# Loads of a sketched attention and channel mix: weights ahead, v pieces of batches 1 and 2 between halves of the next batch's keys and queries

## The chip, the cores and the metric

The kernel runs on one core of one Trainium2 chip, in one launch. Its time is the device time of an execution in microseconds; a version is told by the median of several executions. One further execution is taken by the hardware profiler, which lists what every engine did and when; the span is the time from its first instruction to its last.

## The reference

Polysketch attention, followed by an RWKV channel mix on its output. There are 4 batches, 4 heads, 1088 positions, a head size of 32; the sketch has 8 rows, so a feature vector has 64 entries.

```python
def phi(x):                                   # S1, S2: 8 x 32
    a = np.einsum('rd,bhsd->bhsr', S1, x)
    b = np.einsum('rd,bhsd->bhsr', S2, x)
    return np.einsum('bhsi,bhsj->bhsij', a, b).reshape(*x.shape[:-1], r * r)
q_p, k_p = (phi(q), phi(k))
kv = np.einsum('bhsf,bhsd->bhfd', k_p, v)     # needs all of k and v of a batch
z = np.sum(k_p, axis=2)
num = np.einsum('bhsf,bhfd->bhsd', q_p, kv)
den = np.einsum('bhsf,bhf->bhs', q_p, z)[..., None] + 1e-06
x = num / den                                 # heads side by side: 4 x 1088 x 128
xk = mu_k * x + (1.0 - mu_k) * x_prev         # x_prev: x one position earlier
xr = mu_r * x + (1.0 - mu_r) * x_prev
k = np.maximum(xk @ w_k, 0.0)                 # w_k: 128 x 1024
v = k * k @ w_v                               # w_v: 1024 x 128
out = 1.0 / (1.0 + np.exp(-(xr @ w_r))) * v   # w_r: 128 x 128
```

Inputs and output are float32.

## The kernel before

The four batches go one after the other through the attention and then through the channel mix, and the stages of different batches are interleaved by hand. The positions of a head are cut into 32 runs of 34 (`U`); with 4 heads that makes the 128 partitions, so a tile of keys or queries of one batch is 128 x (34 x 32). Three things written out as text set the order of the work.

**The loads.** `LOADS` (lines 31 to 34) is a list of entries: what is loaded, `@`, and the queue that issues it (S is SyncE, A is ScalarE). `load` (line 128) turns an entry into DMAs: `k` and `q` of a batch (line 139) go whole, in two halves of 17 columns each, or in the part that `UH` (line 126) names; `v` (line 143) goes in four pieces, `v10` to `v13` for batch 1, each into 32 of the 128 partitions of `vin`; `w0` is `w_k` (line 146), `w1` is `w_v` (line 148), `w2` is `w_r` (line 150). All loads but the four smallest come from the SyncE queue, in the order of the list. The list is issued at line 160, ahead of all compute.

**The order of compute.** `ORDER` (lines 35 to 66) lists every task for all engines; each engine carries out its own tasks in that order. A task has its arguments behind points, `@` gives the PSUM banks that it writes, and the last letter the engine (V VectorE, A ScalarE, G GpSimd, P VectorE reading PSUM). `^` ties a GpSimd task to the end of a VectorE task.

**The tasks that read the loads:**
- `turn.k.b` and `turn.q.b` (line 252) transpose keys and queries on VectorE, 32 x 32 blocks at a time, into `kT` and `qT`, of which there are two each. Batch 0 is turned in two parts; for the keys of batches 1 and 2 (`WHOLE_K`) there are two transposes (line 261); the keys of batch 3 and the queries of batches 1 to 3 are one transpose (line 264), which reads all 34 columns.
- `kproj` (line 268) multiplies the turned keys with the sketch on TensorE (line 274 for batches 1 and 2, line 280 for 0 and 3); `abev` copies it out of PSUM; `kp` (line 298) forms the 64 features.
- `zmm` (line 307), `wmm` (line 315) and `wsq` make the weights of the query projection `abw` (lines 365 to 386).
- `kvmm` (line 327) sums features times v over the positions: the one reader of `vin`.
- `wset.0` (line 244, GpSimd) scales `w_k` into bf16, `wset.1` (line 246) casts `w_v`, `wset.2` (lines 248, 249) scales `w_r`; `wset.2` is tied to the end of `xs.0` on VectorE.
- `xmm` (lines 496, 513) gives the attention's output, `f1` (line 553), `relu`, `sq`, `f2` (line 586), `rr` (line 599), `sig`, `fin` are the channel mix.

Around the two places that read batch 1's v and batch 3's keys, TensorE's list is `kproj.2.0, f1.1.0, kvmm.1, zmm.2, kproj.3.0, kproj.3.1, wmm.2, f1.0.1`, and VectorE's is `turn.q.2, abev.2.1, turn.k.3, kp.2.0, abev.3.1, wsq.2`.

`zz` (line 175) are matmuls on a tile of zeros, whose result nobody reads. The outputs are stored from line 622 and 618.

Of the kernel before, what the change touches and what calls it, by code (L numbers as in the profile page):

```python
# [20 lines left out]
SIGMOID = mybir.ActivationFunctionType.Sigmoid  # L21
# [7 lines left out]
WHOLE_K = (1, 2)  # L29
WHOLE_Q = (0, 1, 2)  # L30
LOADS = """
S0@A S1@S m0@A m1@A k00@S k01@S q01@S q00@S v00@S v01@S v02@S v03@S k1@S q1@S w0@S v10@S v11@S v12@S v13@S w2@S w1@S
k2@S q2@S k3@S q3@S v20@S v21@S v22@S v23@S v30@S v31@S v32@S v33@S
"""
ORDER = """
turn.k.0.0.V smm.0@0 cset.0 turn.k.0.1.V zz.5@7 kproj.0.1@0 abev.0.1.A kproj.0.0@1 turn.q.0.1.V cset.4.G abev.0.0.V
# [37 lines left out]
def kernel(  # L74
# [14 lines left out]
    nc = tc.nc  # L89
    B, H, S, D = q.shape  # L90
# [4 lines left out]
    U = S // 32  # L95
# [14 lines left out]
    kin = [const.tile([P, U * D], F32, name=f"k{b}") for b in range(B)]  # L110

    X32 = [const.tile([P, U + 1, 32], F32, name=f"qx{b}") for b in range(B)]
    qin = [x[:, 1:, :].rearrange("p u d -> p (u d)") for x in X32]
# [9 lines left out]
    omu = const.tile([P, 2], F32, name="omu")  # L123
    rat = const.tile([P, 1], F32, name="rat")
    tmp = const.tile([P, 1], F32, name="tmp")
    UH = {"k": {"": (0, U), "0": (0, 18), "1": (18, U)}, "q": {"": (0, U), "0": (0, 16), "1": (16, U)}}

    def load(what, eng):
        e = nc.sync if eng == "S" else nc.scalar if eng == "A" else nc.gpsimd
        x, b, i = what[0], int(what[1]), what[2:]  # L130
        if x == "S":
            e.dma_start(S16[R * b:R * b + R, :], S2 if b else S1)
        elif x == "m":
            e.dma_start(mu_row[b:b + 1, :], (moe_mu_r if b else moe_mu_k).rearrange("d -> () d"))
        elif x in "kq":
            src = (k if x == "k" else q)[b].rearrange("h (a u) d -> (h a) (u d)", u=U)
            lo, hi = UH[x][i]
            for lo, hi in ((lo, hi),) if i else ((0, U // 2), (U // 2, U)):
                e.dma_start((kin if x == "k" else qin)[b][:, lo * D:hi * D], src[:, lo * D:hi * D])
        elif x == "v":  # L140
            c = int(i)
            u, n = CU[c]
            e.dma_start(vin[b][32 * c:32 * c + 32, :, :n, :].rearrange("p h m d -> p h (m d)"),
                        v[b].rearrange("h (a u) d -> h a u d", u=U)[:, :, u:u + n, :].rearrange("h a m d -> a h (m d)"))
        elif x == "w" and b == 0:
            e.dma_start(wk_f[:, :, :DFF // 2], moe_w_k.rearrange("p (y f) -> p y f", y=2))
        elif x == "w" and b == 1:
            e.dma_start(wv_f[:, :, :DFF // 2], moe_w_v.rearrange("(p y c) d -> p y (c d)", y=2, c=NC // 2))
        else:
            e.dma_start(wr_f[:], moe_w_r)  # L150

    warm = const.tile([R, 1], F32, name="warm")
# [4 lines left out]
    nc.vector.memset(warm[:], 0.0)  # L157
    for b in range(B):
        nc.vector.memset(vin[b][64:, :, 8, :], 0.0)
    for entry in LOADS.split():  # L160
        load(*entry.split("@"))
    nc.scalar.activation(warm[:], warm[:], SIGMOID)


    ident = const.tile([P, P], F32, name="ident")
# [86 lines left out]
    def turn(x, b, y, eng="V"):  # L252
        lo, hi = UH[x][str(y) if y < 2 else ""]
        t, src = (kT, kin) if x == "k" else (qT, qin)
        t = t[b % 2][:].rearrange("p u a -> p (u a)")
        if x == "k" and b in WHOLE_K:

            for c in (0, 2):
                u, n = CU[c]
                if lo <= u < hi:  # L260
                    nc.vector.transpose(_ap(t, [[32, 2], [P, n], [1, 32]], 32 * c),
                                        src[b][:, D * u:D * (u + 2 * n)].rearrange("p (c m d) -> p c m d", c=2, m=n))
        else:
            nc.vector.transpose(t[:, 32 * lo:32 * hi], src[b][:, D * lo:D * hi])  # L264
# [412 lines left out]
```

## Time and profile before

| | us |
|---|---|
| three executions | 82.67, 80.83, 82.23 |
| their median | 82.23 |
| the profiled execution, its own time | 81.55 |
| its span in the profile | 79.8 |

Busy time in the span: TensorE 73.0 us (91%), weight loads 54.1, VectorE 64.0 (80%), ScalarE 58.5 (73%), GpSimd 43.2 (54%).

How the profile is read: PE is TensorE's matmuls, PEld its weight loads, which overlap with them; DVE is VectorE, ACT ScalarE, POOL GpSimd, SP SyncE, and a q behind an engine's name is its queue of instructions, which issues DMAs. A row of the timeline has the start, the duration, the engine, the line of the kernel, the operation, what it writes and reads, the shapes, and in brackets how long the engine stood idle before it and what ended that. A row of the chain has start, duration and what the end of the program depended on in that time. A row of a table by stretches has, after the stretch, busy time and number of instructions for each engine, the granted TensorE clock, the mean share in which the 16 DMA engines were busy, and GB/s. A row of waits has who waited for what, the total, how often, and the longest. A row of DMA issues has the size of one and the median time to landing.

### The profile page before, as it was taken

The page shows a single profiled execution, that of the slowest core. Times are in us where ns is not written, and L with a number is a line of the kernel's source. Part 1 is how long each engine was busy: PE and PEld are TensorE (multiplying, and loading weights), DVE is VectorE, ACT ScalarE, POOL GpSimd, SP SyncE. Part 2 cuts the span into 40 slices and gives each one's busy share as a digit, 9 for nine tenths or more (in the row PEclk, how much of TensorE's full clock was granted, in tenths as well). Part 3 has the DMA queues.
Part 4 walks back from the last instruction along what each step waited for, and adds up shares of the span by engine and source line. Part 5 has one row for each costly group of instructions (what it writes and reads, how often), then busy time and mean ns, then how long its engine had stood idle before and what let it go on. Part 6 is the DMA issues. An engine that isn't in the chain of part 4 may idle for free.

```text
span 79.8 us, 3602 instructions
## 1 busy us (share of the span) xinstructions
PE 73.0 (91%) x1558; PEld 54.1 (68%) x1558; DVE 64.0 (80%) x121; ACT 58.5 (73%) x87; POOL 43.2 (54%) x55
## 2 busy tenths in 40 slices
PE   5998699999999999999999999999999999999700
PEld 2236387797757795849586877987676776889600
DVE  5272858669799989937999798899999999799900
ACT  0701013048899999895999799999999899999500
POOL 6030392999679999973910990974940920000600
PEclk9999999999999999999999999999999999999999
DMA  0899999999999962000041000050054002420280
GB/s 1 268 281 227 253 360 341 192 227 314 397 403 248 205 151 83 8 0 8 0 105 36 11 0 0 8 133 11 5 136 126 4 0 72 125 74 0 80 246 7
DMA packets 9876, 10.26 MB, mean 129 GB/s; under 512 B 1122, under 2 KB 7268, under 8 KB 9860
## 3 DMA queue, kind: packets, MB, share of 16 engines
q1 hardware_dynamic: 9488, 9.77, 44.4%
q8 instruction: 12, 0.20, 1.1%
q0 software_dynamic: 64, 0.13, 0.7%
q10 hardware_dynamic: 308, 0.13, 0.6%
q14 instruction: 4, 0.03, 0.1%
HBM read 7.80 MB, written 2.23 MB: 126 GB/s over the span
## 4 chain that ended last, share of the span: by engine, by line
PE 83%; DMA 7%; issue 2%; SPq 1%; DVE 1%; DVEq 0%
PE ps L586 19%; PE ps L553 19%; DMA qx<-in_q_dram 7%; PE ps L327 6%; PE ps L513 6%; PE ps L386 5%; PE ps L599 5%; PE ps L274 5%; PE ps L175 3%; PE ps L369 2%; PE ps L451 2%; PE ps L479 1%; PE ps L307 1%; PE ps L496 1%; PE ps L280 1%
## 5 line engine op out<-in xcount | busy, mean ns | idle before, releaser
L561 ACT ACTIVATE k<-ps 128x1024 bf16<-128x1024 f32 (+1 forms) x36 | 33.3, 1010 | 0.6 <-PE ps L553 0.6
L586 PEld LDWEIGHTS <-k 128*128 128x128 bf16 x272 | 16.9, 98 | 4.1 <-issue 0.4
L586 PE MATMUL ps<-wv,k 128*128 128x128 bf16 x272 | 19.1, 219 | 0.0
L553 PE MATMUL ps<-xk,wk 128*128 128x512 bf16 x64 | 17.6, 379 | 0.0
L576 DVE TENSOR_TENSOR k<-k 128x1024 bf16<-128x1024 bf16 (+1 forms) x23 | 14.2, 648 | 0.9 <-ACT k L561 0.9
L431 POOL TENSOR_TENSOR qp<-an,abw 128x1024 f32<-128x1024 f32 (+1 forms) x5 | 10.2, 2047 | 1.7 <-DVE qp L431 1.7
L298 POOL TENSOR_TENSOR kp<-ab 128x1024 f32<-128x1024 f32 (+1 forms) x5 | 10.6, 2134 | 0.0
L576 POOL TENSOR_TENSOR k<-k 128x1024 bf16<-128x1024 bf16 x4 | 7.6, 1893 | 5.3 <-DVE qx L204 3.0
L574 ACT ACTIVATE k<-k 128x1024 bf16<-128x1024 bf16 x9 | 9.6, 1073 | 0.0
L175 PE MATMUL ps<-zero 128*128 128x512 bf16 x22 | 8.1, 489 | 1.0 <-DVE warm L157 1.0
L553 PEld LDWEIGHTS <-wk 128*128 128x128 bf16 x72 | 6.0, 100 | 2.6 <-DVE XT L532 0.3
L440 DVE STREAM_TRANSPOSE qpT<-qp 128x1152 f32<-128x1152 f32 (+1 forms) x6 | 7.6, 1294 | 0.1
L264 DVE STREAM_TRANSPOSE qT<-qx 128x1088 f32<-128x1088 f32 (+2 forms) x5 | 5.3, 1068 | 1.9 <-DMA qx<-in_q_dram 1.9
L622 POOL DMA_DIRECT2D out_dram<-k x2 | 1.3, 663 | 9.8 <-DVE k L612 9.8
L202 ACT COPY ab<-ps 128x320 f32<-128x320 f32 (+1 forms) x5 | 2.1, 419 | 5.5 <-PE ps L280 2.9
L529 DVE SCALAR_TENSOR_TENSOR xk<-ps,rat,qx 128x512 bf16<-128x512 f32 x8 | 5.7, 746 | 0.5 <-ACT qx L202 0.5
L607 ACT ACTIVATE k<-ps 128x512 f32<-128x512 f32 x8 | 5.2, 644 | 0.6 <-PE ps L599 0.6
L612 DVE TENSOR_TENSOR k<-ps,k 128x512 f32<-128x512 f32 x8 | 5.3, 668 | 0.1
L513 PE MATMUL ps<-qpT,kvt 32*32 32x256 f32 x192 | 5.2, 385 | 0.1
L327 PEld LDWEIGHTS ps<-kp,v 128*32 128x32 f32 x288 | 4.3, 110 | 1.3 <-issue 0.4
L327 PE MATMUL ps<-kp,v 128*32 128x64 f32 x288 | 4.9, 220 | 0.1
L386 PE MATMUL ps<-SQ,qT 128*32 128x96 f32 x192 | 5.0, 247 | 0.0
(107 smaller groups left out, 118.5 us busy)
## 6 DMA issues: line engine op xcount, KB each, us to landing
out_dram<-k SPq DMA_DIRECT2D x28, 64.0 KB, 1.7
k<-in_k_dram SPq DMA_DIRECT2D x6, 272.0 KB, 6.9
qx<-in_q_dram SPq DMA_DIRECT2D x6, 272.0 KB, 6.3
v<-in_v_dram SPq DMA_DIRECT2D x8, 144.0 KB, 6.5
v<-in_v_dram SPq DMA_DIRECT2D x8, 128.0 KB, 5.5
wk_f<-in_moe_w_k_dram SPq DMA_DIRECT2D x1, 512.0 KB
wv_f<-in_moe_w_v_dram SPq DMA_DIRECT2D x1, 512.0 KB, 7.8
k<-in_k_dram SPq DMA_DIRECT2D x1, 288.0 KB, 2.8
```

Source lines behind the costliest of these rows:

```text
L175: nc.tensor.matmul(PS[:, banks[0], :], zero[:], _ap(zero[:], [[0, 4], [1, P]]), skip_group_check=True)
L298: e.tensor_mul(o[:], _ap(a_, list(a_.ap[1:]) + [[0, R]]), _ap(b_, [list(b_.ap[1]), [0, R], list(b_.ap[2])]))
L327: nc.tensor.matmul(o[32 * h:32 * h + 32, :], vin[b][:, h, m, :], sb["kp", b, j][:, 4 * (m - KG[j][0]) + h].rearrange("p i j -> p (i j)"), ...
L386: nc.tensor.matmul(d, qT[b % 2][:, 16 * g + (quad(t) + c if TURN[b] == "O" else 4 * c + t), :], SQ[b][:], skip_group_check=True, tile_posi ...
L431: e.tensor_mul(o[:, :s1 - s0], _ap(a_, list(a_.ap[1:]) + [[0, R]]), _ap(b_, [list(b_.ap[1]), [0, R], list(b_.ap[2])]))
L440: nc.vector.transpose(sb["qpT", b][:].rearrange("p s y a -> p (s y a)")[:, F * s0:F * s1], sb["qp", b, g][:].rearrange("p s i j -> p (s i ...
L513: nc.tensor.matmul(o[32 * h:32 * h + 32, c, :], sb["kvt", b][y, f, 32 * h:32 * h + 32], m, start=(f == 0), stop=(f == 1), skip_group_check ...
L553: nc.tensor.matmul(h[:, c, :], wk[:, 2 * cp + c].rearrange("p y f -> p (y f)"), x, skip_group_check=True)
L561: nc.scalar.activation(o[:, :, :size(g)], h, RELU)
L574: nc.scalar.activation(o[:, :, :n], k1[:, :, :n], SQUARE)
L576: (nc.gpsimd if eng == "G" else nc.vector).tensor_mul(o[:, :, :n], k1[:, :, :n], k1[:, :, :n])
L586: nc.tensor.matmul(o[:, i * P:i * P + P], k2[:, c, i * P:i * P + P], wv[:, 2 * cp + c, :], start=(cp == 0 and c == 0 and i == 0), stop=(cp ...
```

## The change

`LOADS` is in another order from `w0` on: `w2` and `w1` stand right behind `w0`, ahead of batch 1's v; the v pieces of batch 1 stand one by one ahead of the halves of batch 2's keys and queries, those of batch 2 ahead of the halves of batch 3's; batch 3's v stays last. So that the halves can be named in the list, `UH` gets `a` and `b`, and the loop over two halves in `load` goes. The issuing loop runs twice, the second time for entries that begin with v and end in A, of which the list has none; the warm-up activation stands between the two.

```diff
 LOADS = """
-S0@A S1@S m0@A m1@A k00@S k01@S q01@S q00@S v00@S v01@S v02@S v03@S k1@S q1@S w0@S v10@S v11@S v12@S v13@S w2@S w1@S
-k2@S q2@S k3@S q3@S v20@S v21@S v22@S v23@S v30@S v31@S v32@S v33@S
+S0@A S1@S m0@A m1@A k00@S k01@S q01@S q00@S v00@S v01@S v02@S v03@S k1a@S k1b@S q1a@S q1b@S w0@S w2@S w1@S v10@S k2a@S
+v11@S k2b@S v12@S q2a@S v13@S q2b@S v20@S k3a@S v21@S k3b@S v22@S q3a@S v23@S q3b@S v30@S v31@S v32@S v33@S
 """
...
-    UH = {"k": {"": (0, U), "0": (0, 18), "1": (18, U)}, "q": {"": (0, U), "0": (0, 16), "1": (16, U)}}
+    UH = {"k": {"": (0, U), "0": (0, 18), "1": (18, U), "a": (0, 17), "b": (17, U)},
+          "q": {"": (0, U), "0": (0, 16), "1": (16, U), "a": (0, 17), "b": (17, U)}}
...
             lo, hi = UH[x][i]
-            for lo, hi in ((lo, hi),) if i else ((0, U // 2), (U // 2, U)):
-                e.dma_start((kin if x == "k" else qin)[b][:, lo * D:hi * D], src[:, lo * D:hi * D])
+            e.dma_start((kin if x == "k" else qin)[b][:, lo * D:hi * D], src[:, lo * D:hi * D])
...
-    for entry in LOADS.split():
-        load(*entry.split("@"))
-    nc.scalar.activation(warm[:], warm[:], SIGMOID)
+
+    for late in (0, 1):
+        for entry in LOADS.split():
+            if late == (entry[0] == "v" and entry.endswith("A")):
+                load(*entry.split("@"))
+        if not late:
+            nc.scalar.activation(warm[:], warm[:], SIGMOID)
```

## The prediction

> **What bounds the kernel now.** I read the page's span and chain first, then the engines' busy time over the stretch that the chain holds.
>
> ```profile
> span 79.8 us, 3602 instructions
> ```
>
> ```profile
> PE 83%; DMA 7%; issue 2%; SPq 1%; DVE 1%; DVEq 0%
> ```
>
> ```profile
> 2.07 5.41 DMA qx<-in_q_dram
> ```
>
> ```profile
> 8.71:75.35 66.64, 66.31 (x1463) 51.06 (x1463) 59.34 (x105) 56.67 (x84) 41.15 (x37) 1.00 0.43 119
> ```
>
> The chain that ended last is TensorE's. From 8.71 us, when batch 0's data is in, to 75.35 us TensorE is busy for 66.31 of 66.64 us, at a granted clock of 1.00 (the third column from the right). So only two things can move the end: TensorE work (the diff touches none), or a wait of TensorE that is not there now. The 7% of DMA in the chain is the first query half of batch 0, from 2.07 us; everything up to and with `w0` is issued in the old order, so that stays. What is left to ask is whether each moved load still lands ahead of its reader.
>
> How loads land: the transfers from the SP queue take turns on the same DMA engines, and these are full while the inputs come in (page, DMA share and rate in 40 slices of 2 us).
>
> ```profile
> DMA  0899999999999962000041000050054002420280
> GB/s 1 268 281 227 253 360 341 192 227 314 397 403 248 205 151 83 8 0 8 0 105 36 11 0 0 8 133 11 5 136 126 4 0 72 125 74 0 80 246 7
> ```
>
> The share is 9 up to about 28 us, but the rate falls from 400 to under 200 where v pieces move. A table by stretches (columns: PE, PEld, DVE, ACT, POOL busy, clock, DMA share, GB/s) shows it:
>
> ```profile
> 8.00:10.00 2.00, 1.29 (x24) 0.72 (x24) 1.75 (x7) 0.18 (x1) 0.82 (x4) 1.00 1.09 252
> 14.00:18.00 4.00, 4.00 (x34) 3.44 (x33) 2.57 (x6) 1.06 (x5) 4.00 (x4) 1.00 1.11 208
> 19.00:24.00 5.00, 5.00 (x149) 3.31 (x149) 4.44 (x11) 4.45 (x10) 3.81 (x5) 1.00 1.06 397
> 25.00:28.00 3.00, 3.00 (x58) 2.58 (x58) 2.96 (x5) 3.00 (x6) 2.92 (x3) 1.00 0.98 194
> ```
>
> From 19 to 24 us nearly only halves of keys and queries move: 397 GB/s. From 25 to 28 us it is nearly all v pieces: 194. From 8 to 10 us halves of batch 1's keys run beside v of batch 0: 252. From 14 to 18 us weights run beside v of batch 1: 208.
>
> **What the change moves.** Sizes, from the DMA issues:
>
> ```profile
> k<-in_k_dram SPq DMA_DIRECT2D x6, 272.0 KB, 6.9
> qx<-in_q_dram SPq DMA_DIRECT2D x6, 272.0 KB, 6.3
> v<-in_v_dram SPq DMA_DIRECT2D x8, 144.0 KB, 6.5
> v<-in_v_dram SPq DMA_DIRECT2D x8, 128.0 KB, 5.5
> wk_f<-in_moe_w_k_dram SPq DMA_DIRECT2D x1, 512.0 KB
> wv_f<-in_moe_w_v_dram SPq DMA_DIRECT2D x1, 512.0 KB, 7.8
> ```
>
> ```profile
> wr_f<-in_moe_w_r_dram SPq DMA_DIRECT2D x1, 64.0 KB, 7.2
> ```
>
> No transfer is added, removed or resized: the new names `a` and `b` cut a batch at 17 of 34 columns, where the old loop cut it. The second loop over LOADS selects entries that begin with v and end in A; there are none, so it issues nothing. Only the order changes. Counting KB from `w0` on (old, new), up to and with each load: w2 1120, 576; w1 1632, 1088; v13 1056, 2448; k2b 2176, 1920; q2b 2720, 2720; k3b 3264, 3552; q3b 3808, 4352; v33 4896, 4896. So the weights and k2 come earlier, q2 stays, batch 1's v comes much later, and k3 and q3 get two and four v pieces more ahead of them.
>
> The SP queue itself: k2b is the ninth load counted from `w0` with `w0` as the first, and its issue waited for `w0` to land; the v31 issue at 26.22 waited in the same way for the load eight before it, which is k3b.
>
> ```profile
> SPq L139 <- DMA wk_f<-in_moe_w_k_dram: 2.0, 1, 2.0
> ```
>
> ```profile
> 16.71 0.33 SPq L139 DMA_DIRECT2D k<-in_k_dram  x1
> ```
>
> ```profile
> SPq L143 <- DMA k<-in_k_dram: 0.5, 1, 0.5
> ```
>
> ```profile
> 26.22 0.31 SPq L143 DMA_DIRECT2D v<-in_v_dram  x1
> ```
>
> Eight loads in flight, then, and these rows give two landings: w0 at 16.7 and k3b at 26.2. After the change k3b's issue waits for k2b; with seven loads ahead of it still under way the engines do not run dry, so bytes and rate decide, not the queue.
>
> Reader by reader:
>
> ```profile
> 18.51 2.18 POOL L210 TENSOR_SCALAR wk<-wk_f,omu 128x1024 bf16<-128x1024 f32 x1
> 21.32 0.37 POOL L210 TENSOR_SCALAR wr<-wr_f,mu 128x128 bf16<-128x128 f32 x1 [0.64 <-DVE qx L204]
> ```
>
> ```profile
> 21.99 1.04 POOL L204 CAST wv<-wv_f 128x1024 bf16<-128x1024 f32 x1
> ```
>
> Weights: w0 landed 1.8 us before its reader. The reader of w2 waits 0.64 us for VectorE (the tie to `xs.0`), not for the DMA, and w1's reader follows w2's at once. Earlier weights: 0 us.
>
> ```profile
> 23.32 0.28 DVE L532 SCALAR_TENSOR_TENSOR XT<-ps,rat,qx 128x64 bf16<-128x64 f32 x1
> 23.51 1.36 DVE L261 STREAM_TRANSPOSE kT<-k 128x576 f32<-128x576 f32 x2
> ```
>
> k2: its turn at 23.51 starts as VectorE comes free, without a wait, so an earlier k2 gains 0. Now the part that can cost:
>
> ```profile
> 25.55 1.25 DVE L264 STREAM_TRANSPOSE qT<-qx 128x1088 f32<-128x1088 f32 x1
> 26.72 0.39 DVE L204 COPY ab<-ps 128x256 f32<-128x256 f32 x1
> 27.03 1.28 DVE L264 STREAM_TRANSPOSE kT<-k 128x1088 f32<-128x1088 f32 x1
> ...
> 29.99 0.42 DVE L204 COPY ab<-ps 128x256 f32<-128x256 f32 x1 [0.30 <-PE ps L280]
> ...
> 33.34 1.29 DVE L264 STREAM_TRANSPOSE qT<-qx 128x1088 f32<-128x1088 f32 x1
> 36.17 0.88 DVE L204 COPY qx<-ps 128x512 f32<-128x512 f32 x2 [1.54 <-ACT k L574]
> ```
>
> `turn.k.3` is one transpose that needs both halves of k3. It starts at 27.03, right behind the copy of 26.72, while k3b has been there since 26.2: 0.83 us of cover on VectorE. It ends at 28.31. Its reader on TensorE is `kproj.3.0` (line 280):
>
> ```profile
> 27.59 1.14 PE ps L327 x72
> ...
> 28.86 1.04 PE ps L280 x70
> ...
> 42.64 1.23 PE ps L327 x74
> ```
>
> ```profile
> 28.67 0.26 PE L280 MATMUL ps<-SK,kT 128*32 128x64 f32 x3
> ```
>
> The first of it starts at 28.67, so 28.67 - 28.31 = 0.36 us more of cover. k3b may land up to 27.03 + 0.36 = 27.4 before TensorE waits; behind that, each microsecond is a microsecond, because everything behind `kproj.3.0` on TensorE stands in one queue.
>
> When does k3b land? The v price is not shown for this mixture, so from both sides. Low: from w0's landing to k3b's, 2752 KB (2.82 MB) took 9.5 us now, 297 GB/s; 3040 KB (3.11 MB) at that average take 10.5 us: 27.2, no wait. Two v pieces at the rate of v alone: 288 KB (0.295 MB) / 194 = 1.5 us: 26.2 + 1.5 = 27.7. By a mixed rate: w2 and w1, 576 KB (0.59 MB) at 397, are in at 16.7 + 1.5 = 18.2; then 2464 KB (2.52 MB) at the 252 of keys beside v are 10.0 us: 28.2. High: at the 208 of weights beside v, 12.1 us: 30.3. The nearest row is that of keys beside v, but it also holds the last pieces of v0 alone; between 27.7 and 28.2 I take 28.0. TensorE then waits 28.0 - 27.4 = **0.6 us** ahead of `kproj.3.0`.
>
> The v rate has a reason in the Trainium skill (SBUF — State Buffer, section "Door 1: The DMA port swizzle"): a transfer into 32 partitions reaches 8 of 16 ports, an asymptote of 8 x 27.2 = 218 GB/s; the 194 here agrees. By that rule alone the two pieces would be an estimated 1.4 us and k3b would land at 27.6, a wait of 0.2.
>
> Where the stall goes: VectorE's later work moves by about 1 us, TensorE by 0.6. VectorE has idle 0.30 before the copy at 29.99 and 1.54 before 36.17 to take up the difference; I add nothing. The other late loads: v13 ends 1360 KB (1.39 MB) behind w1, 5.5 us at 252, so 23.7 (24.9 at 208), and its reader `kvmm.1` starts at 27.59: 0. q2b 1632 KB (1.67 MB) behind w1: 24.8 against 25.55: 0. q3b 3264 KB (3.34 MB): 31.5 against 33.34: 0. v2 and v3 end with the same total, some ten microseconds before line 327 at 42.64: 0.
>
> Sum: 0.6 us on the profiled execution, 81.55 + 0.6 = 82.15 us (span 79.8 + 0.6 = 80.4, and 1.75 around it as now). The median shown, 82.23, lies 0.7 above that execution, so there the sum is 82.8. The middle of the four times known (80.83, 81.55, 82.23, 82.67) is 81.89; with 0.6 I give **82.4 us**.
>
> **Rivals.**
> 1. Nothing waits: k3b lands by 27.4, as at the average rate of 297. For: total bytes and the full engines stay. Against: that average holds only four v pieces ahead of k3b and the new one six. Time: 81.9 on the middle of the times.
> 2. Slow mixture, the other side. Halves and v pieces interleaved run at the mixed rate throughout, so that all of batch 2 and 3 slows, not just by two pieces. Place: `turn.k.3`, then `kproj.3.0`. Price at 208: (30.3 - 27.4) = 2.9 us, 84.8 us; at 230, 2.52 MB take 11.0 us, landing 29.2, +1.8, 83.7. It decides from a landing of 27.4 + 1.64 = 29.0 (2% of 82 us, about what a measurement of this kernel can tell from no change), that is from a rate under 2.52 / (29.0 - 18.2) = 233 GB/s. For: each stretch with v in it shows 194 to 252. Against: in 19 to 24 us the clean halves run at 397, and they are two thirds of the bytes.
> 3. The weights are worth something: were the 0.64 us ahead of the weight's scaling really a wait for w2, it would be won: 81.89 - 0.64 = 81.25. Against: the releaser is VectorE by name, and TensorE was not idle there.
>
> **How the numbers follow.** Forecast (k3b at 27.5 to 28.5, +0.1 to +1.1) 0.45; rival 1 0.25; rival 2 0.25; rival 3 0.05. Slower by over 2%: rather more than half of rival 2, with some scatter of the times, 0.17. Faster by over 2%: no case reaches it, since TensorE has 0.33 us idle in all; only scatter, 0.04. Within 2%: 0.79. Range: from rival 3, 81.25, to rival 2 at 225 GB/s (11.2 us, landing 29.4, +2.0), 83.9: 81.2 to 83.9.
>
> **What would show it.** Right: no idle of TensorE up to 28.6; VectorE idle ahead of `turn.k.3` put down to a DMA of k, about 1 us; TensorE idle ahead of line 280 of some 0.6 us, released by VectorE's kT; a rate of 230 to 300 GB/s from 19 to 28 us where it was 397, then 194; the stretch behind 31 us unchanged in length. Step by step wrong: `turn.k.3` without a wait (rival 1); `turn.q.2` waiting for its DMA as well and k3b behind 29 (rival 2); line 327 for batch 1 waiting for v. A TensorE wait at any other place, or a shorter stretch of 66.6 us, would make the whole reading wrong.

## The result and the profile after

The changed kernel takes 82.69 us (median of four executions, 82.62 to 83.06), the one before 81.53 (four, 80.42 to 82.67). The ratio is 1.0263, with a 95% interval of 1.0206 to 1.0320; it leaves disturbed executions out and so is not the quotient of these medians. Run once more on another occasion, beside 29 executions of before, the changed kernel stood at 1.0184 (1.0112 to 1.0255). So the change costs 1.5 to 2.1 us.

The page of the changed kernel: span, shares of the chain that ended last, and the DMA engines in 40 slices.

```profile
span 81.3 us, 3593 instructions
...
DMA  0899999999999997000032000031045002430280
GB/s 1 275 294 214 269 380 339 280 247 253 237 236 245 254 194 152 16 0 8 0 83 57 10 0 0 8 96 46 0 113 143 11 0 61 118 88 0 71 242 14
...
PE 53%; DMA 26%; SPq 7%; DVE 5%; issue 3%; ACT 1%; DVEq 0%
```

The span is 1.5 us longer. The chain has gone over from TensorE to a load: DMA has 26% of it where it had 7%. The rate, which rose to 400 GB/s between 18 and 24 us, now lies between 236 and 254 from 16 to 28 us, and the last loads end nearly 2 us later (33.7 against 31.9). The middle of the chain, in order of time (start, duration, what):

```profile
13.44 7.92 DMA k<-in_k_dram
...
21.38 6.84 DMA k<-in_k_dram
...
28.32 1.32 DVE kT L268
...
29.68 1.21 PE ps L284 x72
```

Read from the end: `kproj.3` (now line 284) waited for VectorE's transpose `turn.k.3`, this one for k3b, issued at 21.38, and this issue for k2b, issued at 13.44, which is the load eight places ahead of it. With seven more under way the DMA engines stayed full meanwhile (share 1.08 from 18.2 to 28.2 us, shown below), so what counts is how long the bytes ahead of k3b take. VectorE and TensorE at this place:

```profile
25.30 1.25 DVE L268 STREAM_TRANSPOSE qT<-qx 128x1088 f32<-128x1088 f32 x1
26.48 0.39 DVE L208 COPY ab<-ps 128x256 f32<-128x256 f32 x1
28.32 1.31 DVE L268 STREAM_TRANSPOSE kT<-k 128x1088 f32<-128x1088 f32 x1 [1.46 <-DMA k<-in_k_dram]
29.55 1.45 DVE L302 TENSOR_TENSOR kp<-ab,ps 128x1280 f32<-128x1280 f32 x1
30.96 0.43 DVE L208 COPY ab<-ps 128x256 f32<-128x256 f32 x1
```

```profile
28.30 0.35 PE L311 MATMUL ps<-ab 128*32 128x32 f32 x18
29.68 1.21 PE L284 MATMUL ps<-SK,kT 128*32 128x64 f32 x72 [1.03 <-DVE kT L268]
```

The queries of batch 2 at 25.30 still go without a wait. k3 is waited for: VectorE stands 1.46 us, TensorE 1.03 us. One more wait is new in this execution, in the middle of `kvmm`, and the profile names nothing that ends it:

```profile
45.48 1.21 PE L331 MATMUL ps<-kp,v 128*32 128x64 f32 x70 [0.58 <-issue]
```

Matched matmul by matmul, the changed kernel is 0.24 us ahead of before up to `kproj.3.0`, then 1.01 behind, and 1.57 behind from this wait to the end. So 1.25 us are lost at k3 and 0.58 at line 331.

### The profile page after: what moved, and what is told of

The parts are those of the page before. It is cut to its first block, busy times and chain, and to the rows that moved or that the text cites. A ratio compares the mean times of both kernels' runs of the same rounds, so it can differ in the third digit from the quotient of the medians.

```text
span 81.3 us, 3593 instructions
## 1 busy us (share of the span) xinstructions
PE 72.8 (90%) x1549; PEld 54.2 (67%) x1558; DVE 64.0 (79%) x121; ACT 58.6 (72%) x87; POOL 43.3 (53%) x55
## 4 chain that ended last, share of the span: by engine, by line
PE 53%; DMA 26%; SPq 7%; DVE 5%; issue 3%; ACT 1%; DVEq 0%
DMA k<-in_k_dram 18%; PE ps L590 17%; PE ps L557 14%; DMA qx<-in_q_dram 8%; PE ps L517 6%; PE ps L603 4%; PE ps L390 3%; PE ps L331 3%; SPq L139 2%; DVE xk L533 2%; DVE kT L268 2%; PE ps L284 1%; SPq L148 1%; SPq L143 1%; PE ps L349 1%
## 5 line engine op out<-in xcount | busy, mean ns | idle before, releaser
L557 PE MATMUL ps<-xk,wk 128*128 128x512 bf16 x55 | 16.1, 379 | 0.4 <-issue 0.2
L268 DVE STREAM_TRANSPOSE kT<-k 128x576 f32<-128x576 f32 (+2 forms) x3 | 2.8, 927 | 3.0 <-DMA k<-in_k_dram 3.0
```

Source lines behind the costliest of these rows:

```text
L557: nc.tensor.matmul(h[:, c, :], wk[:, 2 * cp + c].rearrange("p y f -> p (y f)"), x, skip_group_check=True)
```

## The experiments

Theory: k3 comes too late for `kproj.3.0`, because two v pieces of batch 2 stand ahead of it, and TensorE has nothing else to do. Rivals: the interleaving slows all loads; the weights' new place; the new waits that no load ends.

### Batch 2's v behind q3 again

```diff
-... v20 k3a v21 k3b v22 q3a v23 q3b v30 v31 v32 v33
+... k3a k3b q3a q3b v20 v21 v22 v23 v30 v31 v32 v33
```

> The new order, but batch 2's v stands behind q3 again, so that k3 has four v pieces ahead of it and not six; v of batch 1 still stands between the halves of batch 2, weights first. Theory (k3b lands too late for kproj.3.0): 2176 KB (2.23 MB) behind the weights at the 250 GB/s of the new profile land k3b at 18.2 + 8.9 = 27.1, so TensorE's wait of 1.03 us ahead of line 284 goes, to 0 to 0.1, and the time is that of before within 0.5 us. Rival (interleaving itself costs, by late batch 1 v or a late batch 2): line 284 is without a wait but the time stays over 1 us above before. Second rival (half a microsecond is a wait for nothing in the middle of line 331, whatever the loads do): 0.5 us stays.

Ratio to before 0.9833 (0.9739 to 0.9927) from few executions; in a second run of the same kernel

> The changed kernel with batch 2's v behind q3, as in e1_k3_first, once more for its time: first look 0.983 from few executions. Theory: no wait at line 284, nothing else gained by the weights or by batch 1's v between the halves: ratio 0.99 to 1.0. Rival (the interleaving of batch 1's v brings something of its own): under 0.988.

0.9975 (0.9930 to 1.0019). In the second profile the load eight places behind k3b is issued, upon k3b's landing, at 24.67, and neither VectorE nor TensorE waits:

```profile
24.67 0.74 SPq L143 DMA_DIRECT2D v<-in_v_dram  x1
```

```profile
27.08 1.28 DVE L268 STREAM_TRANSPOSE kT<-k 128x1088 f32<-128x1088 f32 x1
```

```profile
28.72 0.26 PE L284 MATMUL ps<-SK,kT 128*32 128x64 f32 x3
```

The loss is gone, with v of batch 1 still between the halves of batch 2. So it is the second half of the change, batch 2's v between the halves of batch 3, that costs; of it v20 and v21 stand ahead of k3b. k3b came 2.4 us earlier than expected (1.3 in the first profile), and no later than the 26.2 of before, without any interleaving: the rate of 250 GB/s that I had taken over from the changed kernel is not the interleaving's. The gain of the first run was not repeated.

### The weights alone

```diff
-w0 v10 v11 v12 v13 w2 w1 k2 q2 ...
+w0 w2 w1 v10 v11 v12 v13 k2a k2b q2a q2b ...
```

> Only the two weights are moved ahead of batch 1's v; the rest in the order of before. Theory: k3b has the same 3264 KB ahead of it as before and lands at 26.2 within 0.5; time of before within 0.5 us. Rival (weights first bring something, or cost something): a difference of over 0.6 us either way.

0.9925 (0.9888 to 0.9961): 0.6 us under before, at the edge of what was set as a difference. No reader of a weight waits for a load in either profile, and the kernels below that also have the weights first stand at 0.9956 to 0.9989. The weights' place costs nothing; whether it brings a few tenths stays open.

### The same place, in blocks

```diff
-... v10 k2a v11 k2b v12 q2a v13 q2b v20 k3a v21 k3b ...
+... v10 v11 v12 v13 k2a k2b q2a q2b v20 v21 k3a k3b ...
```

> The same loads ahead of k3b as in the new order (3552 KB), but in blocks: four v pieces of batch 1, then k2 and q2 whole, then two v pieces of batch 2, then k3. If the place alone costs (v pieces at 194 GB/s, halves alone at 397): k3b at 26.2 + 1.5 = 27.7, a wait of 0.3 us, about 0.3 us over before. If the mixture slows the halves: k3b here well before the new order's 28.2, by 0.5 us or more. If blocks and mixture are the same: 28.2 and about 1 us of wait.

The four times spread from 82.03 to 85.43 (median 83.88), so no ratio is read from them. The profile decides:

```profile
28.42 1.31 DVE L268 STREAM_TRANSPOSE kT<-k 128x1088 f32<-128x1088 f32 x1 [1.15 <-DMA k<-in_k_dram]
```

```profile
18.20:28.20 10.00, 9.98 (x222) 7.11 (x224) 8.32 (x16) 9.44 (x17) 8.54 (x9) 1.00 1.03 253
```

```profile
18.20:28.20 10.00, 9.95 (x249) 7.30 (x251) 8.06 (x16) 9.45 (x17) 8.54 (x9) 1.00 1.08 245
```

The first two fences are the blocks, the third the changed kernel, over the same ten microseconds. k3 turns at 28.42 against 28.32, at 253 against 245 GB/s. Blocks and mixture are the same: going one by one as such costs nothing, and the place alone is dearer than the 1.5 us that I had worked out for it. Counted from the landing of the weights, k3b takes 10.3 us in the blocks and 10.1 in the changed kernel, against 7.1 and 8.0 in the two profiles with batch 2's v behind q3.

### Four pieces ahead in place of two

```diff
-... v20 k3a v21 k3b v22 q3a v23 q3b v30 ...
+... v20 v22 k3a v21 v23 k3b q3a q3b v30 ...
```

> The new order with all four v pieces of batch 2 ahead of k3b (two more than in the new order, 256 KB). Theory: 2720 KB (2.79 MB) behind the weights at 250 GB/s land k3b at 29.3, 1.1 us later than in the new order; TensorE's wait ahead of line 284 grows from 1.03 to about 2.1 us and the time by about 1.1 us. Rival (something else than k3 sets the loss): the time stays that of the new order within 0.4 us.

```profile
28.29 1.31 DVE L268 STREAM_TRANSPOSE kT<-k 128x1088 f32<-128x1088 f32 x1 [2.31 <-DMA k<-in_k_dram]
```

```profile
29.65 1.21 PE L284 MATMUL ps<-SK,kT 128*32 128x64 f32 x72 [1.88 <-DVE kT L268]
```

Ratio 1.0152 (1.0096 to 1.0209). TensorE's wait grew to 1.88 us, nearly as expected, but for another reason: it came to this place 0.9 us earlier (batch 0's queries landed at 6.4 us, not 7.1), and k3 was no later, 28.29. The weights were in 0.6 us earlier than in the changed kernel as well (17.6 against 18.1), so the two further pieces cost some 0.6 us and not the 1.1 expected. Nor did the time grow by 1.1 us: 1.0152 lies by the 1.0184 of the changed kernel, which is the sign that was set for the rival. The longer wait is TensorE's own head start, lost again; k3 came no later. The experiment had changed two things at once, the number of pieces and their order (0, 2, 1, 3); a later one changes the order alone.

### The changed kernel again

> The changed kernel itself once more, beside more runs of before on one chip. Theory: the end of k3's loading sets TensorE's restart at line 284, so an early or late landing of batch 0's queries (6.4 to 7.5 us in the profiles so far) does not reach the end; k3b lands at 28.2 within 0.4, TensorE restarts at 29.7 within 0.4, and the scatter of the times stays under 0.7 us where before scatters over 2 us. The 0.58 us in the middle of line 331 is a matter of the single execution: here 0.2 to 0.35 as in the others. Ratio to before 1.015 to 1.025. Rival (a fixed loss at both places): both waits come back, 1.0 and 0.6, and the ratio is 1.026 or more.

```profile
28.17 1.31 DVE L268 STREAM_TRANSPOSE kT<-k 128x1088 f32<-128x1088 f32 x1 [1.45 <-DMA k<-in_k_dram]
```

```profile
29.53 1.21 PE L284 MATMUL ps<-SK,kT 128*32 128x64 f32 x72 [1.03 <-DVE kT L268]
...
32.82 0.25 PE L385 MATMUL ps<-SQ,qT 128*32 128x24 f32 x5 [0.48 <-issue]
```

1.0184 (1.0112 to 1.0255). The wait for k3 is back to the hundredth. Matched as above, 1.25 us are lost there again: TensorE is 0.39 us ahead of before at line 311 and 0.86 behind at line 284. The wait at line 331 is not back; one of 0.48 us stands at line 385 instead. The scatter was 81.86 to 84.48, so that part of the expectation fell.

### TensorE does other work first

```diff
-turn.k.3.2.V kproj.3.0@3 kp.2.0.P
-kproj.3.1@5 relu.1.0.A zev.2.A wmm.2 f1.0.1@01 sq.0.0.A kvev.1.A kvt.1 abev.3.1.V
+turn.k.3.2.V
+relu.1.0.A zev.2.A kvev.1.A f1.0.1@01 wmm.2 kvt.1 kproj.3.0@3 kp.2.0.P kproj.3.1@5 sq.0.0.A abev.3.1.V
```

> The new order of loads, but TensorE carries out f1.0.1, wmm.2 and kvt.1 ahead of kproj.3.0 (about 1.0 us of work that it did behind it), and ScalarE kvev.1 ahead of sq.0.0. No work is added or removed. Theory: k3b lands at 28.2 as before, VectorE's transpose ends at 29.6, TensorE reaches line 284 at about 29.7 to 30.0 and waits for 0 to 0.2 us; the loss goes, time within 0.6 us of before. Rival (the loads slow the stretch in another way): 1 us stays, at other places.

```profile
27.35 1.31 DVE L268 STREAM_TRANSPOSE kT<-k 128x1088 f32<-128x1088 f32 x1 [1.35 <-DMA k<-in_k_dram]
```

```profile
28.80 1.21 PE L284 MATMUL ps<-SK,kT 128*32 128x64 f32 x72
...
30.75 0.21 PE L385 MATMUL ps<-SQ,qT 128*32 128x24 f32 x2 [0.28 <-DVE SQ L322]
31.17 0.25 PE L385 MATMUL ps<-SQ,qT 128*32 128x24 f32 x5 [0.21 <-issue]
```

VectorE still waits 1.35 us for k3, TensorE no longer does at line 284; it waits 0.28 us at line 385 for what VectorE makes late. Ratio 1.0088 (1.0037 to 1.0139) against 1.0184 (1.0112 to 1.0255): about 0.8 us of 1.5 come back, though the intervals overlap a little. One expectation was missed. k3b, with the changed kernel's own list of loads, landed at 27.3 and not at 28.2, as the issue that it released shows:

```profile
27.28 0.31 SPq L143 DMA_DIRECT2D v<-in_v_dram  x1
```

So the trace does not show TensorE covered against a landing at 28.2. It is also of the fastest of the twelve executions, 81.07 us with a median of 81.97. In it TensorE is 1.10 us ahead of before at line 311 and 0.49 at its last matmul, so about 0.6 us go without a wait for k3. That VectorE's wait costs little while TensorE has other work is shown; what makes up the rest is not.

### v pieces into all partitions

```diff
-e.dma_start(vin[b][32 * c:32 * c + 32, :, :n, :]..., v[b]...[:, :, u:u + n, :]...)
+e.dma_start(vin[b][:, c, :n, :]..., v[b]...[:, u * D:(u + n) * D])      # batches 1 to 3
```

> The new order, with each v piece of batches 1 to 3 written to all 128 partitions (one head's columns) in place of 32 partitions and four heads: the same bytes and the same 128 packets of 1152 or 1024 bytes, so v lies in other places and the output is not the reference's. Theory (a v piece is dear because it goes into a quarter of the partitions): it moves at the rate of the halves, 350 GB/s or more; k3b lands at 18.1 + 2.52 MB / 0.35 = 25.3, no wait at line 284, the time is that of before or up to 0.7 us under it. Rival (it is dear for its small packets or for where it is read): the rate stays near 250 GB/s, k3b at 28.2, the wait of 1.0 us stays.

The changed kernel, then this one, from 14 to 18 us, and this one's transpose of k3:

```profile
14.00:18.00 4.00, 4.00 (x35) 3.55 (x35) 2.57 (x5) 1.24 (x4) 4.00 (x3) 1.00 1.06 268
```

```profile
14.00:18.00 4.00, 4.00 (x36) 3.69 (x35) 2.57 (x5) 1.56 (x4) 4.00 (x4) 1.00 1.04 382
```

```profile
26.46 1.28 DVE L272 STREAM_TRANSPOSE kT<-k 128x1088 f32<-128x1088 f32 x1
```

The same bytes are read, in packets of the same sizes, and the stream moves at 382 GB/s in place of 268, with the DMA engines as full (1.04 and 1.06); k3b lands at 23.2 (the issue that it released stands at 23.21), and nobody waits. Ratio to before 0.9936 (0.9884 to 0.9988). A v piece is dear because it is written into a quarter of the partitions; only where the packets go, and with it their order, was changed. That is the rule of the Trainium skill which the prediction set beside its sum (SBUF — State Buffer, "Door 1: The DMA port swizzle"); the rate alone, 194 GB/s, had agreed with it but could have had other reasons.

### The new order, neighbours in different halves

```diff
-... v10 k2a v11 k2b v12 q2a v13 q2b v20 k3a v21 k3b v22 q3a v23 q3b v30 v31 v32 v33
+... v10 k2a v12 k2b v11 q2a v13 q2b v20 k3a v22 k3b v21 q3a v23 q3b v30 v32 v31 v33
```

> The new order with the v pieces of each batch taken in the order 0, 2, 1, 3, so that the two pieces of batch 2 ahead of k3b write to different halves of the partitions (0 to 31 and 64 to 95) and not both to the first. k3b has 16 KB less ahead of it, otherwise all stands as in the new order. Theory (a piece into 32 partitions is slow by where it writes, and two neighbours in different halves share the time): k3b lands 0.5 to 1.2 us earlier, at 27.0 to 27.6, the wait at line 284 falls from 1.03 to 0.2 or less with batch 0 as late as in the first profile, and the ratio to before falls from 1.018 or more to 1.00 to 1.01. Rival (halves between the pieces already spread the writes; the early restart of the four-ahead run was only an early batch 0): landing 28.0 to 28.3, wait of 1 us, ratio 1.015 to 1.026.

```profile
27.46 1.31 DVE L268 STREAM_TRANSPOSE kT<-k 128x1088 f32<-128x1088 f32 x1 [0.54 <-DMA k<-in_k_dram]
```

```profile
28.83 1.21 PE L284 MATMUL ps<-SK,kT 128*32 128x64 f32 x72
```

```profile
18.20:28.20 10.00, 10.00 (x246) 7.31 (x248) 8.86 (x17) 9.46 (x17) 8.55 (x9) 1.00 1.07 269
```

Against the first profile of the changed kernel, k3 turns 0.86 us earlier, TensorE's wait falls to 0.1 us, the rate rises from 245 to 269 GB/s, and the ratio is 1.0105 (1.0060 to 1.0150). This is about what was expected, and still it does not show that the order of the pieces does it. The changed kernel's own list landed k3b at 28.2 and 28.1 in its two profiles, but at 27.3 in the run with TensorE's other order, a little earlier than here (27.4), at this rate:

```profile
18.20:28.20 10.00, 9.85 (x251) 7.28 (x253) 8.05 (x16) 9.57 (x17) 8.54 (x9) 1.00 1.07 258
```

The intervals of the ratios, to 1.0150 here and from 1.0112 for the changed kernel, overlap as well. Counted from the landing of the weights, k3b takes 9.4 us here and 9.8 to 10.1 in those three profiles, so a few tenths are possible; one profile cannot tell them from scatter. The next section has a second test of this order, which speaks against it.

### Two tries at a faster start

In the profiles TensorE's long run starts when batch 0's queries are in, anywhere from 5.9 to 7.5 us. Two kernels set loads of k1 between these queries and batch 0's v; one further had the pieces in the order 0, 2, 1, 3. The line with the minus is the list of the weights-only kernel.

```diff
-... q00 v00 v01 v02 v03 k1a k1b q1a q1b w0 w2 w1 v10 v11 v12 v13 k2a ...
+... q00 k1a k1b v00 v01 v02 v03 q1a q1b ...                       # f5
+... q00 k1a v00 v01 v02 v03 k1b q1a q1b ...                       # g1; g2 with 0, 2, 1, 3
```

> The order of the weights-only run (w2 and w1 behind w0, batch 1's v whole), with batch 0's v behind k1 instead of ahead of it. Theory: batch 0's queries land late because v pieces run beside them (2048-byte packets take 84 ns alone and over 200 beside v); with k1 behind them q01 lands at 6.3 and q00 at 7.3 in place of 7.5 and 8.8, TensorE starts line 311 some 0.7 to 1.2 us earlier, and the time is 0.5 to 1 us under before, if v0 still lands before line 331 at 11.7 to 12.5. Rival (v0 comes too late): it lands at about 12.6, line 331 of batch 0 waits, and nothing is gained. Second rival (the late queries have another cause): q01 stays between 6.4 and 7.5.

> The weights-only order with one half of k1 ahead of batch 0's v and the other behind it. Theory: one half behind the queries is enough to keep v pieces away from them (q01 at 6.1 to 6.5), and v0 lands 0.7 us earlier than with both halves, at about 11.2, so line 331 of batch 0 does not wait; TensorE runs from 7.5 to 7.9 without a gap and the time is 0.6 to 1.0 us under before (ratio 0.988 to 0.993). Rival (the queries' landing scatters for other reasons): the time is that of the weights-only run, 0.9925.

> As g1_half_k1_first, with the four v pieces of each batch in the order 0, 2, 1, 3, so that neighbours in the queue write to different halves of the 128 partitions. Theory (pieces are dear because 32 partitions take half the rate, and two neighbours in different halves can share the time): stretches of v alone move at over 230 GB/s in place of 194, v33 lands about 1 us earlier, k3b about 0.5 us; the time the same as g1_half_k1_first within 0.4 us, since nothing waits for them. Rival (the engines go through the pieces in step, one piece at a time): rates and landings stay.

```profile
12.12 1.21 PE L331 MATMUL ps<-kp,v 128*32 128x64 f32 x72 [0.93 <-DMA v<-in_v_dram]
```

With both halves of k1 ahead (f5) the queries were in at 6.1, but v of batch 0 was late by 0.93 us: 0.9989 (0.9942 to 1.0035). With one half (g1) 0.9973 (0.9928 to 1.0019), and the queries came at 7.5 in its profile. Three profiles of the changed kernel's list have them at 7.1, 6.3 and 6.0, so their landing scatters for a reason that the order of these loads doesn't set. With 0, 2, 1, 3 (g2) 0.9956 (0.9908 to 1.0004), as g1. The faster v alone that was expected of g2 did not come. From 25 to 28 us, where nearly all is v, it moves at 223 GB/s; f5, which has the pieces in the order 0, 1, 2, 3, at 233, and the weights-only kernel at 215 (below: weights-only, f5, g2). From k3b's landing to that of the last v piece f5 and g2 both take 6.0 us.

```profile
25.00:28.00 3.00, 3.00 (x112) 2.58 (x114) 3.00 (x4) 3.00 (x5) 2.92 (x3) 1.00 1.07 215
```

```profile
25.00:28.00 3.00, 3.00 (x85) 2.58 (x88) 3.00 (x5) 3.00 (x5) 2.92 (x3) 1.00 1.05 233
```

```profile
25.00:28.00 3.00, 3.00 (x108) 2.56 (x111) 3.00 (x4) 3.00 (x5) 2.92 (x3) 0.95 0.94 223
```

No kernel that computes the reference beats before by more than 1% in a run with many executions.

## Why the prediction was right or wrong

- **TensorE's chain, and loads matter through their readers alone: right.** The chain changed over exactly where k3 was late, and moving TensorE's work ahead of that place gave about half of the loss back without touching a load, though k3 also came 0.9 us earlier in that profile.
- **Earlier weights and k2 worth nothing: right** within 0.6 us. **q2 and batch 1's v without a wait: right**; line 331 for batch 1 and the transpose at 25.30 do not wait for a load.
- **k3b at 28.0: right, at 28.2 and 28.1, with 27.3 in a third profile of the same list.** Of the two bounds the mixed rate held: 252 GB/s was taken, and 245, 251 and 258 were measured in these three from 18.2 to 28.2 us. The other, two pieces at the 194 of v alone, was too cheap: 1.5 us in the sum. From the weights' landing k3b took 7.1 and 8.0 us with batch 2's v at the back and 9.8 to 10.1 with two pieces of it ahead, so these cost some 2 to 3 us. Why they cost that much, and the next two only some 0.6, is not shown; going one by one is not the reason (the blocks), and the order 0, 2, 1, 3 is not shown to help. That 28.0 came out so near has luck in it: one list scatters by 0.9 us, and with batch 2's v at the back k3b landed anywhere from 23.7 to 26.2.
- **"k3b may land up to 27.4 before TensorE waits": the step that failed.** The limit was read from an execution in which batch 0 came late (transposed from 7.50). In the profile after it came at 7.13, TensorE's list ran 0.24 us ahead, and the limit lay lower by as much. VectorE's start, 28.32, is 0.3 later than the 28.0 of the sum. Together these take the 0.6 of the sum to nearly 1.2, of the 1.25 us that were lost at this place (1.03 of them show as TensorE's idle time).
- **"I add nothing" behind the stall: right for VectorE, wrong in sum.** VectorE was 1.29 us late at `turn.k.3` and 0.97 at the copy behind `kproj.3`, as TensorE was, so the idle time did take it up. But the changed kernel loses another 0.6 and 0.3 us behind k3 in its two profiles, part of it in waits that nothing in the profile ends (0.58 at line 331, 0.48 at line 385). Such waits are not bound to the new order: the weights-only kernel, which is not slower than before, has 0.20 at line 385 and 0.30 at line 331. The kernel with TensorE's other order and the one with 0, 2, 1, 3 stay 0.7 to 0.9 us over before, with a wait for k3 of 0.1 us at most in the one execution of each that was profiled; the kernel with batch 2's v at the back keeps no loss. Whether k3 comes later in their other executions, or something else in these loads costs, was not found.
- **The numbers.** 82.69 lies in the range, but the forecast band of +0.1 to +1.1 us does not hold a cost of 1.5 to 2.1: right in mechanism, low in size, at k3 (1.25 for 0.6) and behind it (0.3 to 0.6 for nothing). That 82.4 is so near to 82.69 is in part luck, since it stands on 81.89 for before, which took 81.53 here and 81.28 to 81.44 later. Rival 2, slow mixture, named the right place and a larger price, from a rate under 233 GB/s that was not reached; part of its reason is seen, since packets of keys and queries do take longer beside v pieces (last section). "Within 2%" got most of the chance; the two measurements, 2.6% and 1.8%, lie on both sides of that line.

## What to carry to other kernels

When loads are put in another order, work out for each reader how much cover it has, and take that limit from an execution in which everything ahead was early, since cover read from a late one is borrowed. Count a load by where it writes and not by its bytes alone, and take its price from the mixture that it joins: two pieces cost 2 to 3 us here and not the 1.5 of their rate alone. And move only what has slack: batch 2's v had over ten microseconds at the back of the queue and was put ahead of keys that had 0.8.

## What was unexpected of the hardware

- The same 128 packets of 1152 or 1024 bytes move at 382 GB/s into 128 partitions and hold the stream at 268 into 32 (14 to 18 us), in one queue with weights and halves. The packets of 1152 bytes take 51 ns there (median) and 78 into 32 partitions, and the packets of keys and queries beside them, of 2176 bytes, 88 and 151: narrow pieces slow their neighbours too.
- Halves and v pieces one by one, or in blocks, come out the same: 245 and 253 GB/s, k3 at 28.32 and 28.42.
- The trace marks the landing of a load sixteen times, once for each DMA engine, and the last one counts. Half of k3b's marks were there at 23.4 us before the change and the last at 26.2; after it 26.5 and 28.2; with v into all partitions 22.7 and 23.2. So a mean rate tells such a landing only to within some microseconds; no experiment here tells why one engine lags.
- TensorE waits of up to 0.58 us without a releaser stand at the same few instructions and vary between profiles; no experiment here tells their cause.
